# Token weights staged further ahead in a Fourier filter and mixer kernel, with readerless matmuls, joint copies and adds on VectorE

## The chip, the cores and the metric

The kernel runs on one core of a Trainium2 chip. The metric is the device time of one execution in microseconds (us). Beside the profile of one execution there are the times of three plain runs.

## The reference

The input `x` has 8 batches of 3008 rows (the sequence) and 256 columns. Stage one multiplies its Fourier transform along the sequence by a complex filter; stage two is a mixer, first over the sequence ("token"), then over the columns ("channel"), with a residual in between. All is float32, except that the four mixer weights arrive as 64-bit floats.

```python
def _attn_ref(x, filt_r, filt_i):
    X = np.fft.rfft(x, axis=1)
    Y = X * (filt_r + 1j * filt_i)[None, :, :]
    return np.fft.irfft(Y, n=x.shape[1], axis=1).astype(np.float32)

def _moe_ref(x, w_tok1, w_tok2, w_ch1, w_ch2):
    xt = x.transpose(0, 2, 1)
    h = np.maximum(xt @ w_tok1, 0.0) @ w_tok2        # (3008, 256) and (256, 3008)
    u = x + h.transpose(0, 2, 1)
    h2 = np.maximum(u @ w_ch1, 0.0) @ w_ch2          # (256, 1536) and (1536, 256)
    return (u + h2).astype(np.float32)
```

## The kernel before

The transform of length 3008 is split as 47 x 64. A first set of matmuls works over the 64, a second set over the 47 for each of 32 row pairs k, then the filter product and the same two steps backwards. The last inverse step is not done by itself: its matrix (`wai`, and `wai_t` for the weights) is applied together with the mixer's token product. The mixer's matmuls over 1536 channels use a seven-product scheme of block sums, so that VectorE (DVE) and GpSimd (POOL) add blocks around TensorE's (PE's) matmuls. PE does 128 x 128 stationary by up to 512 moving float32 columns. The program is written in the order in which each engine runs it; each engine waits only for what its next instruction needs. Batch 0 is brought up first, in a stage of its own; after that batches follow each other with the filter of the next beside the mixer of the present one.

What the first stage does, in the order of the program:

- **Row transform of batch 0.** Twelve x tiles are multiplied by `wa0` (L534) and copied by ScalarE (ACT) into the tile `turned` (L537). After the sixth and the twelfth, eight DVE transposes each (L651) turn the rows in it. `turned` and `wa0` share one tile of the pool `wcp`, whose single place is later taken by the channel weights (`both`, the list `chan`).
- **Pair loop**, 33 steps over k = 0..32. `b_unit(k)` multiplies row k of `turned` by a table (L666), and DVE multiplies the result by the filter (L671) once ACT has copied the filter's second half (`filt_double`, L255). `bi_unit(k-1)` does two matmuls of 256 columns (L680) into one PSUM bank; ACT copies the result (L690, helper `by_block`), and after each odd k ACT issues the write to `g_tmp` (L687). ACT also turns the tables (L262, L263). Filter loads go out on POOL's queue (L243 to L250) eight k ahead, tables (L583) on SP's.
- **Weight tiles**, 38 in all: 12 of `w_tok1`, 14 of `w_tok2` (indices 12 to 25), 2 of `w_ch1`, and 10 more (`LAST`) of the channel weights. A 64-bit tile is loaded into a staging place (`stage`; L347 on SP for the first twelve, L362 and L394, L405 on POOL), scaled by ACT (L283), and rebuilt as a float32 part `top` and a small `rest` by four DVE instructions (L285, L286, L289, L291). For `w_tok1` and the first six tiles of `w_tok2` PE then adds the two by two matmuls that accumulate (L329 with `top`, L330 with `rest`, helper `on_chip`) and ACT copies the sum out (L332); for the others DVE adds (L318). In the pair loop every two k end one tile; `convert_end` counts it in `ended` and calls `fill`.
- **How far ahead tiles begin.** `fill(5)` begins loads while fewer than five tiles (four for `LAST`) are begun and not ended; `pause` holds it for the last k of the loop. Staging places come from a list: 7 buffers `t4`, then six buffers (`u`, `t`, `v`, two each) in turn for indices 12 to 27, then `t2` and `t3`. A load into a place that was used before waits until DVE has read the older tile.
- **Token sums.** `t4_load` reads rows of `g_tmp` back (L782, on SP, three of the last ones on POOL), and 96 matmul records (L788) sum over the sequence. Then come the first units of u (L874, L882), which need all fourteen `w_tok2` tiles, and the mixer items (L975, L985, L1004, L1022 on PE; L953 is the helper of all DVE adds), between which the remaining tiles are converted and POOL combines channel weights (L382 to L386). The filter of batch 1 runs beside them: its `z_tmp` writes (L545), reads (L661, L662), filter loads (L229 to L235) and products (L707).

The matmuls of the pair loop and the adding of the two parts, before the change:

```python
            for i, p in enumerate(prods.pop(k)):
                wi = turn_i[:, k // WC % 4, k % WC] if i else wbs[k // WC][:, TI:TI + 2 * KR:2, k % WC]
                nc.tensor.matmul(ps[0:KR], wi, p, start=(i == 0), stop=(i == 1))
```

Of the kernel before, what the change touches and what calls it, by code (L numbers as in the profile page):

```python
# [10 lines left out]
FP32 = mybir.dt.float32  # L11
I64 = mybir.dt.int64
U32 = mybir.dt.uint32
AF = mybir.ActivationFunctionType
ALU = mybir.AluOpType
# [4 lines left out]
N1 = 47  # L20
N2 = 64
NF = N // 2 + 1
D = 256
P = 128
K2 = 32
A = 24
KR = 4 * A
# [3 lines left out]
NXC = A // XC  # L31
# [4 lines left out]
KC = 2  # L36
KD = 2 * KC
WC = 2
TI = P - 2 * KH + 1
DT = 256  # L40
TC = DT // P
DC = 1536
JT = DC // P
JP = JT // 2
DH = D // P
# [3 lines left out]
NG = 10  # L49
W2G = -(-N2 // NG)  # L50
# [80 lines left out]
def kernel(  # L131
# [11 lines left out]
    nc = tc.nc  # L143
# [23 lines left out]
    wcp = pool("wcp", 1)  # L167
# [6 lines left out]
    t4p = pool("t4p", A // TC4 + 1)  # L174
# [10 lines left out]
    def bank(tag):  # L185
        return (psg if tag == "pg" else psum).tile([P, 512], FP32, tag=tag, name="ps_" + tag)
# [5 lines left out]
    def free_bank():  # L192
        turn.reverse()
        return turn[0]
# [4 lines left out]
    wai_t = glob.tile([P, P], FP32, name="wai_t")  # L199
# [7 lines left out]
    w1 = w1_all[:, 0:A * DT].rearrange("p (a t) -> p a t", t=DT)  # L207
# [3 lines left out]

    w2m = [w2[:, t, 0:7 * 256].rearrange("p (s n) -> p s n", s=7) for t in range(2)]

    turned = wcp.tile([P, K2 * D + P], FP32, tag="wc", name="turned")
    wa0 = turned[:, K2 * D:]
    turned = turned[:, 0:K2 * D].rearrange("p (s d) -> p s d", d=D)
    chan = []


# [46 lines left out]

    early = [(up, "u")] * 2 + [(tp, "t")] * 2 + [(vp, "v")] * 2
    late = [(t2p, "t2"), (t3p, "t3")]
    stages = [(t4p, "t4")] * (A // 2) + (early * 3)[0:TC * W2G + DH] + late * 5

    def stage(n):
        where, tag = stages.pop(0)
        return where.tile([P, n], I64, tag=tag, name="st")

    def halves(st, n, pair):
# [45 lines left out]
    ended = [0]  # L321
    behind, banks = [], ["po%d" % i for i in range(4)]

    def on_chip(stat, top, rest, n, parts):
        banks.append(banks.pop(0))

        def f(tag=banks[0]):
            ps = bank(tag)
            nc.tensor.matmul(ps[:, 0:n], stat, top, start=True, stop=False)  # L329
            nc.tensor.matmul(ps[:, 0:n], stat, rest, start=False, stop=True)  # L330
            for src, dst in parts:
                nc.scalar.copy(out=dst, in_=src(ps))  # L332

        behind.append(f)

    def w1_tile(i):
        st = stage(512)
        rows = moe_w_tok1.rearrange("(n2 n1) t -> n2 n1 t", n1=N1)
        q = nc.sync if i < EARLY else nc.gpsimd
        if 2 * i + 2 == A:  # L340
            nc.gpsimd.memset(st.bitcast(U32)[:, 512:1024], 0)
        for j in range(2):
            a = 2 * i + j
            both = a + 1 < A
            src = bass.AP(tensor=rows.tensor, offset=rows.offset + (A - 1 - a) * DT,
                          ap=[[N1 * DT, N2]] + [[(1 + 2 * a) * DT, 2]] * both + [[1, DT]])
            q.dma_start(st[0:P:1 if both else 2, ts(j, DT)], src)  # L347
        yield

        h = halves(st, 512, spare_pair())  # L350
        yield next(h)
        yield next(h)
        on_chip(wai_t, *next(h), 512, [(lambda v: v, w1[:, 2 * i:2 * i + 2, :].rearrange("p a t -> p (a t)"))])

    def w2_load(i):

# [103 lines left out]
    begun, pause = [0], []  # L460

    def fill(ahead):
        while not pause and begun[0] < len(tiles) and begun[0] < ended[0] + (4 if begun[0] >= len(tiles) - len(LAST) else ahead):
            start()

    def start():
# [5 lines left out]
    xs, ahead = {}, []  # L472
# [92 lines left out]
    def dft(bs):  # L565
# [72 lines left out]
        for i, u in enumerate(() if tiled else todo):  # L638
            if first and i in (0, 2):
                w_load(i // 2)  # L640
            if first and i in (6, 8):
                table_load(i // 2 - 1)
            a_unit(*u)
            if bs != GROUPS[1] or i >= XB:
                more(1)
            yield "a" if i + 1 < len(todo) else "w"
            if first and (i + 1) % (NXC // 2) == 0:

                for d in range(i // (NXC // 2) * P, (i + 1) // (NXC // 2) * P, 16):
                    v = turned.rearrange("p s d -> p d s")[:, d:d + 16, :]  # L650
                    nc.vector.transpose(v, v)  # L651
        t2s, t3s, prods = {}, {}, {}
        def t2_load(c):
            t2s[c] = t2p.tile([P, KD, D], FP32, tag="t2", name="t2")
# [19 lines left out]
        def bi_unit(k):  # L674


            ps = bank(free_bank()).rearrange("p (b d) -> p b d", b=2)[:, 0:nb, :]
            for i, p in enumerate(prods.pop(k)):
                wi = turn_i[:, k // WC % 4, k % WC] if i else wbs[k // WC][:, TI:TI + 2 * KR:2, k % WC]
                nc.tensor.matmul(ps[0:KR], wi, p, start=(i == 0), stop=(i == 1))  # L680
            c, r = divmod(k, KC)
            if r == 0:
                where, tag = (p2p, "p2") if c % 3 == 2 else (t3p, "t3")
                t3s[c] = where.tile([KR, KC, nb, D], FP32, tag=tag, name="t3")
            by_block(t3s[c][:, r], ps[0:KR])
            if r == KC - 1:
                nc.scalar.dma_start(g_d[0][ts(c, KC)].rearrange("k r b d -> r k b d"), t3s.pop(c))  # L687

        def by_block(out, ps):
            nc.scalar.copy(out=out.rearrange("p b (e g i) -> p b g e i", e=DH, i=CW),  # L690
                           in_=ps.rearrange("p b (g e i) -> p b g e i", e=DH, i=CW))
# [695 lines left out]
```

## Time and profile before

| what | value |
|---|---|
| three runs, median (lowest to highest) | 2398.6 us (2395.35 to 2398.96) |
| the profiled execution | 2395.43 us, its span 2393.7 us |
| PE busy over the span | 2356.6 us, 98% |
| DVE, ACT, POOL busy | 1943.6, 688.1, 641.0 us |
| mean granted clock of PE | 0.996 |
| PE busy from 0 to 100, 100 to 200, 200 to 300 us | 82.5, 93.9, 96.2 us |
| DVE, ACT, POOL busy from 60 to 80 us, of 20 | 15.7, 17.7, 17.0 us |
| DMA over the span | 294 MB, mean 123 GB/s |

The page cuts the span into 40 slices of 60 us and gives the busy share of each in tenths. Tables by stretch give, for each engine, the busy time and the number of instructions, then the granted share of PE's clock, the mean busy share of the 16 DMA engines and what they moved in GB/s. A timeline row has the start, the length, the engine, the line, output and input, and in brackets the idle time of the engine ahead of it and what ended that. A row of waits has the total, how often, and the longest. Issuing a DMA is not counted as busy time of the engine that issues it, and a float32 matmul stands as two records.

### The profile page before, as it was taken

The page shows a single profiled execution, that of the slowest core. Times are in us where ns is not written, and L with a number is a line of the kernel's source. Part 1 is how long each engine was busy: PE and PEld are TensorE (multiplying, and loading weights), DVE is VectorE, ACT ScalarE, POOL GpSimd, SP SyncE. Part 2 cuts the span into 40 slices and gives each one's busy share as a digit, 9 for nine tenths or more (in the row PEclk, how much of TensorE's full clock was granted, in tenths as well). Part 3 has the DMA queues.
Part 4 walks back from the last instruction along what each step waited for, and adds up shares of the span by engine and source line. Part 5 has one row for each costly group of instructions (what it writes and reads, how often), then busy time and mean ns, then how long its engine had stood idle before and what let it go on. Part 6 is the DMA issues. An engine that isn't in the chain of part 4 may idle for free.

```text
span 2393.7 us, 36991 instructions
## 1 busy us (share of the span) xinstructions
PE 2356.6 (98%) x13108; PEld 2007.5 (84%) x13108; DVE 1943.6 (81%) x3653; ACT 688.1 (29%) x1339; POOL 641.0 (27%) x1124
## 2 busy tenths in 40 slices
PE   7999999999999999999999999999999999999998
PEld 4667789888898888988888888988889888898887
DVE  7797887888887888878887788788888788877776
ACT  5732222322223222232222222132222322212222
POOL 8485533211211121222111211221121112112121
PEclk8999999999999999999999999999999999999999
DMA  8864446333354333533344333533335433331100
GB/s 228 235 197 134 146 129 223 112 108 94 112 178 134 94 96 110 198 112 95 104 154 153 107 94 104 193 113 108 94 112 177 135 94 97 108 130 33 38 15 21
DMA packets 190423, 294.28 MB, mean 123 GB/s; under 512 B 34444, under 2 KB 124962, under 8 KB 190238
## 3 DMA queue, kind: packets, MB, share of 16 engines
q1 hardware_dynamic: 148750, 231.24, 31.1%
q0 software_dynamic: 34688, 53.83, 8.6%
q10 hardware_dynamic: 6800, 6.85, 0.9%
q8 instruction: 104, 1.70, 0.3%
q14 instruction: 81, 0.66, 0.1%
HBM read 209.06 MB, written 82.72 MB: 122 GB/s over the span
## 4 chain that ended last, share of the span: by engine, by line
PE 93%; DVE 3%; DMA 2%; issue 1%; POOL 1%; ACT 0%; SPq 0%; DVEq 0%; ACTq 0%; POOLq 0%
PE ps_po L1022 35%; PE ps_pg L975 20%; PE ps_pg L1004 15%; PE ps_b L527 3%; PE ps_b L839 3%; PE ps_acc L896 3%; PE ps_pg L527 2%; PE ps_acc L839 2%; PE ps_b L896 2%; PE ps_acc L874 2%; PE ps_b L874 2%; DVE t L953 1%; PE ps_pg L666 1%; DMA x<-in_x_dram 1%; PE ps_b L680 1%
## 5 line engine op out<-in xcount | busy, mean ns | idle before, releaser
L1030 POOL DMA_DIRECT2D out_dram<-r x752 | 408.3, 551 | 1452.1 <-issue 864.0
L1009 ACT ACTIVATE hh<-hh 128x512 f32<-128x512 f32 (+1 forms) x568 | 342.7, 621 | 989.1 <-DVE hh L953 989.1
L953 DVE TENSOR_TENSOR hh<-ps_pg,s 128x512 f32<-128x512 f32 (+3 forms) x852 | 475.4, 585 | 167.2 <-ACT s L978 157.1
L1022 PE MATMUL ps_po<-t,wc 128*128 128x256 f32 (+1 forms) x2296 | 556.4, 379 | 0.8 <-DVE t L953 0.8
L1022 PEld LDWEIGHTS ps_po<-t,wc 128*128 128x128 f32 x2296 | 427.1, 190 | 93.0 <-issue 33.9
L1022 PE MATMUL ps_po<-hh,wc 128*128 128x256 f32 (+1 forms) x1722 | 411.5, 375 | 1.1 <-POOL wc L386 1.1
L975 PE MATMUL ps_pg<-v,wc 128*128 128x256 f32 (+1 forms) x1704 | 406.6, 375 | 0.0
L1022 PEld LDWEIGHTS ps_po<-hh,wc 128*128 128x128 f32 x1722 | 326.8, 190 | 40.2 <-POOL wc L386 1.9
L975 PEld LDWEIGHTS ps_pg<-v,wc 128*128 128x128 f32 x1704 | 323.5, 190 | 36.9 <-DVE v L953 0.4
L1004 PE MATMUL ps_pg<-u,wc 128*128 128x256 f32 (+1 forms) x1136 | 287.7, 376 | 3.3 <-DVE hh L953 3.1
L953 DVE TENSOR_TENSOR t<-t,hh 128x256 f32<-128x256 f32 (+1 forms) x576 | 247.6, 430 | 19.8
L1004 PEld LDWEIGHTS ps_pg<-u,wc 128*128 128x128 f32 x1136 | 213.9, 190 | 32.7 <-DVE hh L953 7.5
L953 DVE TENSOR_TENSOR s<-ps_pg,hh 128x512 f32<-128x512 f32 (+1 forms) x284 | 193.3, 681 | 29.6
L978 ACT COPY s<-ps_pg 128x256 f32<-128x256 f32 (+1 forms) x284 | 104.4, 367 | 326.5 <-PE ps_pg L975 326.4
L953 DVE TENSOR_TENSOR t<-hh 128x512 f32<-128x512 f32 (+1 forms) x288 | 194.4, 675 | 0.6 <-ACT hh L1009 0.6
L975 PE MATMUL ps_pg<-u,wc 128*128 128x256 f32 (+1 forms) x568 | 166.9, 375 | 0.4 <-DVE hh L953 0.4
L1004 PE MATMUL ps_pg<-v,wc 128*128 128x256 f32 (+1 forms) x568 | 166.4, 375 | 0.0
L975 PEld LDWEIGHTS ps_pg<-u,wc 128*128 128x128 f32 x568 | 106.3, 190 | 14.1 <-DVE hh L953 2.1
L1004 PEld LDWEIGHTS ps_pg<-v,wc 128*128 128x128 f32 x568 | 107.3, 190 | 12.7
L953 DVE TENSOR_TENSOR u<-ps_acc,u 128x256 f32<-128x256 f32 (+1 forms) x84 | 46.1, 549 | 72.4 <-PE ps_acc L896 50.2
L953 DVE TENSOR_TENSOR u<-ps_b,u 128x512 f32<-128x512 f32 (+2 forms) x126 | 74.5, 591 | 28.9 <-PE ps_b L896 26.7
L896 PE MATMUL ps_acc<-w 128*128 128x256 f32 (+1 forms) x336 | 85.2, 376 | 0.0
(168 smaller groups left out, 2708.4 us busy)
## 6 DMA issues: line engine op xcount, KB each, us to landing
w<-w_tmp SPq DMA_DIRECT2D x84, 448.0 KB
w<-w_tmp SPq DMA_DIRECT2D x35, 896.0 KB
out_dram<-r POOLq DMA_DIRECT2D x696, 32.0 KB, 3.5
g_tmp<-t SPq DMA_DIRECT2D x112, 192.0 KB
t<-g_tmp SPq DMA_DIRECT2D x42, 512.0 KB
t<-z_tmp SPq DMA_DIRECT2D x196, 96.0 KB
z_tmp<-t SPq DMA_DIRECT2D x72, 256.0 KB
wb<-wbi_t SPq DMA_DIRECT2D x56, 256.0 KB
```

The source lines that it names most:

```text
L527: nc.tensor.matmul(outs(i, j), stat(i, j), mov(i, j), start=True, stop=True)
L666: nc.tensor.matmul(ps, wbs[k // WC][:, 0:2 * P:2, k % WC], turned[:, k, :].unsqueeze(1), start=True, stop=True)
L839: nc.tensor.matmul(ps[:, at], w[:, n], mov, start=(j == 0 and i in (0, 2)), stop=(j == AP - 1 and i >= 5))
L874: nc.tensor.matmul(ps[:, ds(q * P, n)], t4[b, c][:, r, ts(dh, P)], wai[:, 0:n], start=(first and q == 0), stop=(not first and q == 3))
L896: nc.tensor.matmul(ps[:, ds(j * hw, hw)], h1[:, n, :], w2m[m % 2][:, at, 0:hw], start=(i < 2 and j == 0), stop=(j == len(todo) - 1))
L953: nc.vector.tensor_tensor(out=out, in0=in0, in1=in1, op=op)
L975: nc.tensor.matmul(ps[:, 0:hw], chan[0][:, jp, n, :], mov, start=True, stop=True)
L978: nc.scalar.copy(out=s[:, 0], in_=g[0][:, 0, 0:hw])
L1004: nc.tensor.matmul(ps[:, 0:hw], chan[0][:, jp, n, :], mov, start=True, stop=True)
L1009: nc.scalar.activation(out=hs, in_=hs, func=AF.Relu)
L1022: nc.tensor.matmul(po[i][:, j, 0:hw], chan[1][:, jp, n, :], mov, start=(jp == 0 and first == 1), stop=(jp == JP - 1 and last == 1))
L1030: q.dma_start(bass.AP(tensor=ob.tensor, offset=ob.offset + row * D + g * cw, ap=[[N1 * D, 32], [D if h else -D, n], [1, cw]]), blocks[ts(g ...
```

## The change

Five edits, all in the first stage of the program:

- The tile that holds `turned` and `wa0` gets the size of `both` and the name `early_wc`. The staging list now has, after the 7-buffer places of the first twelve tiles, the six buffers once; then three places behind `wa0` in `early_wc` (indices 18 to 20); then five places on top of `turned`, four of its rows each (indices 21 to 25); then two buffers again for the two `w_ch1` tiles. One swap puts the short tile (index 18) into the short third place.
- `fill` has a rule by stretches: four ahead for `LAST`; from twelve begun tiles on, 5 + min(max(ended - 2, 0) // 2, 6) ahead, so 7 at seven ended tiles and 11 from fourteen on; below that, what the caller says.
- `on_chip` can be called without `rest`; for every second tile of `w_tok1` (six of twelve) DVE adds `rest` to `top` in place and PE does one matmul, not two.
- After each of the last eight transposes a matmul of 384 columns reads the slice just turned, with `wa0` as its stationary; nothing reads its result.
- `bi_unit` puts the results for k and k + 1 into the two halves of one PSUM bank, and ACT copies both with one instruction after the second.

```diff
-    turned = wcp.tile([P, K2 * D + P], FP32, tag="wc", name="turned")
-    wa0 = turned[:, K2 * D:]
-    turned = turned[:, 0:K2 * D].rearrange("p (s d) -> p s d", d=D)
+    early_wc = wcp.tile([P, 2 * JP * 7 * P], FP32, tag="wc", name="turned")
+    wa0 = early_wc[:, K2 * D:K2 * D + P]
+    turned = early_wc[:, 0:K2 * D].rearrange("p (s d) -> p s d", d=D)
...
-    stages = [(t4p, "t4")] * (A // 2) + (early * 3)[0:TC * W2G + DH] + late * 5
+    stages = [(t4p, "t4")] * (A // 2) + early + [(early_wc, K2 * D + P + n * NG * N1) for n in (0, 2, 4)]
+    stages += [(early_wc, n * 4 * D) for n in range(5)] + early[0:DH] + late * 5
+    stages[A // 2 + W2G - 1], stages[A // 2 + 8] = stages[A // 2 + 8], stages[A // 2 + W2G - 1]
 
     def stage(n):
         where, tag = stages.pop(0)
+        if where is early_wc:
+            return where[:, ds(tag, min(2 * n, 2 * JP * 7 * P - tag))].bitcast(I64)
         return where.tile([P, n], I64, tag=tag, name="st")
...
-            nc.tensor.matmul(ps[:, 0:n], stat, top, start=True, stop=False)
-            nc.tensor.matmul(ps[:, 0:n], stat, rest, start=False, stop=True)
+            nc.tensor.matmul(ps[:, 0:n], stat, top, start=True, stop=rest is None)
+            if rest is not None:
+                nc.tensor.matmul(ps[:, 0:n], stat, rest, start=False, stop=True)
...
-        on_chip(wai_t, *next(h), 512, [(lambda v: v, w1[:, 2 * i:2 * i + 2, :].rearrange("p a t -> p (a t)"))])
+        top, rest = next(h)
+        if i % 2:
+            nc.vector.tensor_tensor(out=top, in0=top, in1=rest, op=ALU.add)
+            rest = None
+        on_chip(wai_t, top, rest, 512, [(lambda v: v, w1[:, 2 * i:2 * i + 2, :].rearrange("p a t -> p (a t)"))])
...
-        while not pause and begun[0] < len(tiles) and begun[0] < ended[0] + (4 if begun[0] >= len(tiles) - len(LAST) else ahead):
+        while not pause and begun[0] < len(tiles):
+            if begun[0] >= len(tiles) - len(LAST):
+                ahead = 4
+            elif begun[0] >= A // 2:
+                ahead = 5 + min(max(ended[0] - 2, 0) // 2, 6)
+            if begun[0] >= ended[0] + ahead:
+                break
             start()
...
                     nc.vector.transpose(v, v)
+                    if i + 1 == NXC:
+                        nc.tensor.matmul(bank("pg")[:, 0:384], wa0, turned[:, 0:24, d:d + 16], start=True, stop=True)
...
-            ps = bank(free_bank()).rearrange("p (b d) -> p b d", b=2)[:, 0:nb, :]
-            for i, p in enumerate(prods.pop(k)):
-                wi = turn_i[:, k // WC % 4, k % WC] if i else wbs[k // WC][:, TI:TI + 2 * KR:2, k % WC]
-                nc.tensor.matmul(ps[0:KR], wi, p, start=(i == 0), stop=(i == 1))
             c, r = divmod(k, KC)
             if r == 0:
                 where, tag = (p2p, "p2") if c % 3 == 2 else (t3p, "t3")
                 t3s[c] = where.tile([KR, KC, nb, D], FP32, tag=tag, name="t3")
-            by_block(t3s[c][:, r], ps[0:KR])
+                prods["out"] = bank(free_bank()).rearrange("p (r d) -> p r d", r=KC)
+            ps = prods["out"]
+            for i, p in enumerate(prods.pop(k)):
+                wi = turn_i[:, k // WC % 4, k % WC] if i else wbs[k // WC][:, TI:TI + 2 * KR:2, k % WC]
+                nc.tensor.matmul(ps[0:KR, r:r + 1], wi, p, start=(i == 0), stop=(i == 1))
             if r == KC - 1:
+                by_block(t3s[c][:, :, 0], ps[0:KR])
                 nc.scalar.dma_start(g_d[0][ts(c, KC)].rearrange("k r b d -> r k b d"), t3s.pop(c))
```

## The prediction

> **What bounds the kernel now.** I read the page's slices first, then a table by 20 us and by 5 us, then each engine's timeline up to 260 us, last the waits.
>
> ```profile
> PE   7999999999999999999999999999999999999998
> PEclk8999999999999999999999999999999999999999
> ```
> TensorE (PE) is full from the second slice of 60 us on and its clock is down only in the first. All that the change edits lies in the first 190 us, so the gain is bounded by PE's idle time there and by PE work taken out of it. In order of time, from PE's timeline:
>
> ```profile
> 31.44 2.06 PE L666 MATMUL ps_pg<-turned,wb 128*128 128x256 f32 x4 [11.60 <-issue]
> 36.44 1.02 PE L329 MATMUL ps_po<-both,wai_t 128*128 128x512 f32 x2
> 40.79 1.02 PE L329 MATMUL ps_po<-both,wai_t 128*128 128x512 f32 x2
> 111.00 20.96 PE L788 MATMUL ps_b<-t,w 128*128 128x256 f32 x96 [2.08 <-DMA t<-g_tmp]
> 210.85 1.13 PE L1004 MATMUL ps_pg<-u,wc 128*128 128x256 f32 x4 [2.67 <-DVE hh L953]
> ```
> PE waits 11.6 us for the row turns, then runs without a gap through the pair loop (a period of 4.35 us for two rows k and one weight tile, 36.44 to 40.79), and waits for the last `g_tmp` rows at 111.0. That moment, called T0, ends the first stage. One period of ScalarE (ACT) in the loop:
>
> ```profile
> 39.25 0.58 ACT L332 COPY w<-ps_po 128x512 f32<-128x512 f32 x1 [0.40 <-PE ps_b L680]
> 39.73 0.37 ACT L690 COPY t<-ps_b 96x256 f32<-96x256 f32 x1
> 40.12 1.04 ACT L255 COPY filt<-filt 64x1024 f32<-64x1024 f32 x1
> 41.19 0.54 ACT L262 COPY turn_i<-wb 64x192 f32<-64x192 f32 x1
> 41.76 0.56 ACT L263 ACTIVATE turn_i<-wb 64x192 f32<-64x192 f32 x1
> 42.34 0.69 ACT L283 ACTIVATE both<-st 128x512 f32<-128x512 f32 x1
> 42.94 0.35 ACT L690 COPY t<-ps_acc 96x256 f32<-96x256 f32 x1
> 43.31 0.31 ACTq L687 DMA_DIRECT2D g_tmp<-t  x1
> 43.66 0.58 ACT L332 COPY w<-ps_po 128x512 f32<-128x512 f32 x1 [0.38 <-PE ps_b L680]
> ```
> Start to start it is 4.41 us, and the 0.4 "idle" is the DMA issue at 43.31. ACT has no gap at all and falls behind PE by 0.06 us a period: the loop, which looks PE-bound, is ACT-bound as well, and its last `g_tmp` write is issued by ACT at 104.39. The DMA engines and their waits:
>
> ```profile
> 20.00:25.00 5.00, 0.00 (x0) 0.00 (x0) 5.00 (x6) 1.15 (x2) 4.76 (x11) 0.62 0.64 168
> 30.00:35.00 5.00, 3.56 (x8) 2.30 (x9) 3.56 (x6) 0.81 (x2) 4.35 (x9) 0.51 1.04 260
> 90.00:95.00 5.00, 5.00 (x20) 3.90 (x18) 3.48 (x7) 4.51 (x10) 0.54 (x1) 1.00 1.00 330
> ...
> PE ps_po L1022 <- POOL wc L386: 1.1, 2, 0.6
> ACT w L332 <- DMA t<-g_tmp: 1.2, 1, 1.2
> ...
> SPq L782 <- DMA g_tmp<-t: 15.7, 4, 8.6
> ```
> The clock (third number from the end) falls at about 21 us and is back at about 35. DMA (the last two) is full in most rows of 75 to 105 us; a `g_tmp` write then takes so long that SP waits 8.6 us for one, and ACT once waits for an older load to land before it may issue its write.
>
> **The change part by part.** The sum stands against the profiled execution, 2395.43 us (span 2393.7 and 1.7 around it). It is 3.2 under the median of the three runs, 2398.6, and beside the lowest, 2395.35; from the median all totals are 3.2 higher. What a measurement can tell from no change is about 0.2%, 4.8 us.
>
> *Readerless matmuls.* Eight of 384 columns. A 512-column one takes 0.86 (L329 to L330), a 256 one 0.43, so 0.65 each, 1.3 at half clock. The 16 transposes take 17.22 us on VectorE (DVE), 1.08 each, and the last eight free one slice every 1.08; seven matmuls run in PE's 11.6 us of idle time and cost nothing; without that wait they would be 4.6. The eighth needs the last transpose and stands before the first L666: +0.65. Against it, at half clock PE is full from about 24, so the clock should be up before 31, and L666 and L680 take 0.43 rather than 0.9. The first product (DVE, 32.75) stays where it is; the second waits for L286 in any case (34.41). What is left is 0.4 on PE: the first L329 ends its pair at 37.7, not 38.16. If the clock stays low the same point is 0.7 later instead.
>
> *Joint copies.* Two copies of 256 columns (0.39 and 0.37 to the next start) become one of 512; the nearest row is L332, 0.58, and the issue behind must wait for its end: 0.61. ACT's period becomes 4.41 - 0.76 + 0.61 = 4.26. Ends: 0.48 (L332 to its next) and 0.74, no gain. Also the first copy (35.31), which stood ahead of the filter doubling (35.71), goes away, and ACT, idle since 30.84, doubles and turns early. Its first L332 then waits for PE at 37.7, not for its own queue: 37.85 for 39.25, 1.4 earlier (0.25 with the clock low).
>
> *VectorE adds.* Six second matmuls of 0.86 go, 5.2 us of PE in the loop: on average 4.35 becomes 3.92. That is under ACT's 4.26, so it is ACT that sets the period and most of the 5.2 turns into PE waiting. DVE gets six adds of 0.69 (its own L291 at the same size); it idles 0.65 to 0.99 each period ahead of the product that waits for L255, which hides them. Without that idle time they cost 4.1. DVE's mean period would be 3.85.
> The three together: 1.4 at the start and 14 periods and the last copy at 0.15, 2.15. ACT issues the last write at 104.39 - 3.55 = 100.85.
>
> *Tiles begun ahead.* No instruction is added, but their place moves. By the fill rule, with `ended` counting one tile every two k: by the pause, 23 tiles are begun and not 18, and 27 rather than 21 right behind the loop. POOL runs ahead: it issued its last such load at 98.27 and then waited 10.1 us. Places of their own take away waits for buffers there (3.0 and 3.7 and 4.2 us before the loads at 89.25, 93.53 and 98.27), so that about nine more tiles are issued by 89. On POOL the filter loads stand behind up to two more issues of 0.55 each; they go out eight k, 17 us, ahead and land in 4 to 7, so that hides. The three `t<-g_tmp` of POOL stand behind tiles 23 to 26, seven issues of 0.55, in POOL's 10 us wait: nothing. SP's order is unchanged, but its table loads and `g_tmp` reads share the engines. Tiles 21 to 26 are 2.6 MB that ran at 110 to 120: 8 us at 330 GB/s. Free DMA time in the 5 us rows of 60 to 105 is 5.2 (0.72, 0.72, 0.75, 0.99 and 0.78 the rows that are not full), so 2.8 or more may stand before the last write and reads; but the load at 98.27, which stands there now, is gone. I take the middle of 0 and 2.8, a delay of 1.4; the far end is all 2.6 MB at the loop's 230 GB/s, 11.5. T0: 111.0 - 3.55 + 1.4 = 108.85.
>
> *Behind T0.* PE then has 21 us of token sums. DVE converts in order from 102 to 176 and loses 0.72, 1.02 and 2.46 us up to 117 to loads that had not come; with those in place it is over 4 us ahead of PE. So PE's waits of 0.16, 0.55, 0.57 and 0.39 (150 to 185 us, for DVE and for POOL's combines behind DVE) go: 1.67. What is late next is the wait of 2.67 at 210.85, where DVE stands in a filter product that waits for a load. That load follows the last `z_tmp` write, issued at 186.76 beside POOL's `w_tmp` writes (181.45); an earlier POOL gets those out of the way. Between 0 and 2.67 I take half, 1.3. The new `wc` tile may be written only after the last staged tile has been read, which DVE's order gives anyway. Later stages have no PE idle time and no edit.
>
> Sum: 2395.43 - 3.55 + 1.4 - 1.67 - 1.3 = 2390.3. Or: 2388.9 plus the delay.
>
> **The rivals.** *The loop's gain is lost to DMA.* The delay is 2.8 to 6.5: 2391.7 to 2395.4, taken as 2393. For it: the 8.6 us of SP. Against it: 96.26, where a read landed after 2.3 us with two tiles issued in the 7 us before. The clock staying low (1.1 later) also ends here, 2391.4.
>
> *ACT blocked at its own DMA issue; slower.* L687 waits for an older transfer to land (1.2 us with the issue, at 102). If the moved loads stand in front of the writes of the loop's last third, SP's reads behind these land as much later, and ACT waits for them with the loop's last copies queued behind. The price is the delay itself: from 6.5 us on nothing is gained, from 11.3 on it is over 0.2% slower, and at the far end, 11.5, it is 2400.4. For it: DMA full from 75 on, and transfers that land in about the order in which they were issued on whatever queue (tile at 85.67, write at 87.39: both at 95 to 96). Against it: nothing is issued between about 90 and the end of the loop.
>
> *Queues that take turns.* Were the small write and reads served beside the large loads, the delay would be 0: 2388.9. For it: the read at 96.26. Against it: the order of landing just told. The Trainium skill, page DMA: Bandwidth & Descriptors, section Queues, rings and completion order, says that each DMA engine goes round-robin between the queues that have work, a packet at a time; by that rule the last write would not stand behind POOL's tiles and this would be the time. The landings of this trace between 75 and 100 us do not agree with it, so the sum keeps a delay.
>
> **How the numbers follow.** Forecast (delay 1.4, 2390.3) 0.36; queues in turn (2388.9) 0.14; gain lost (2393) 0.31; ACT blocked (2400.4 at its end, some of it under 0.2%) 0.19. Faster by over 0.2% (under 2390.6) is nearly all of the first two, 0.48; slower by over 0.2% the upper part of the last, 0.16; the rest 0.36. The range: low end 2387, the sum with no delay, all of the 2.67 and a cheaper copy; high end 2400, near the far end of the delay. The forecast's own range is 2388 to 2393.
>
> **What would show it.** ACT's starts of L332 4.26 apart and six L329 without L330; PE with small gaps in the loop; eight matmuls of 384 columns at 24 to 32 and the clock up before 31; the last L687 near 100.9 and L788 near 108.9; no PE wait on POOL's L386. Wrong if L687 waits microseconds for a landing, if L788 starts at 111 or later, or if DVE's adds make PE wait at L329 by more than ACT's lead.

## The result, and the profile after

The changed kernel takes 2402.01 us (median of 15 runs, 2399.89 to 2407.32), the kernel before 2395.98 (15 runs beside them, 2394.43 to 2398.96). The ratio is 1.0027, with a 95% interval of 1.002 to 1.0034: slower by 0.27%. The forecast was 2390.3, the range 2387 to 2400; both missed. The profiled run of the changed kernel took 2401.22 us with a span of 2399.4, 5.7 more than the span before. Most lines have moved: L329, L330, L332, L680, L687, L690, L782, L788 and L1022 of before are now L333, L335, L337, L702, L705, L708, L800, L806 and L1040, and L362 and L394, where GpSimd (POOL) issues the loads of the `w_tok2` and `w_ch1` tiles, are L371 and L403. L666, L671, L882, L975 and L1004 are now L683, L688, L900, L993 and L1022, the helper L953 is L971 and the combine L386 is L395; in the runs below some lines stand a few places off these.

From the timeline of TensorE (PE) after (start, length, then the idle time ahead and what ended it):

```profile
31.20 0.88 PE L668 MATMUL ps_pg<-turned 128*128 128x384 f32 x2 [0.20 <-DVE turned L666]
...
36.07 1.02 PE L333 MATMUL ps_po<-both,wai_t 128*128 128x512 f32 x2
...
95.69 0.76 PE L702 MATMUL ps_b<-p,wb 128*96 128x256 f32 x2 [1.81 <-DVE p L688]
...
116.28 22.58 PE L806 MATMUL ps_b<-t,w 128*128 128x256 f32 x96 [7.56 <-issue]
139.55 1.98 PE L900 MATMUL ps_acc<-w,h 128*128 128x512 f32 x4 [0.69 <-ACT h L882]
...
172.62 1.13 PE L1040 MATMUL ps_po<-hh,wc 128*128 128x256 f32 x4 [0.42 <-POOL wc L395]
190.58 0.70 PE L993 MATMUL ps_pg<-u,wc 128*128 128x256 f32 x2 [0.41 <-DVE hh L971]
...
216.03 1.13 PE L1022 MATMUL ps_pg<-u,wc 128*128 128x256 f32 x4 [2.30 <-DVE hh L971]
```

And the line of before that L900 is held against:

```profile
132.64 1.99 PE L882 MATMUL ps_acc<-w,h 128*128 128x512 f32 x4 [0.69 <-ACT h L864]
```

The start is as planned: the readerless matmuls fill the wait, and the loop's first L333 stands at 36.07, 0.37 earlier than before. But T0, the start of the token sums, is 116.28 and not 111.0, and the sums take 22.58 us and not 20.96. These two, 5.28 and 1.62, are the 6.9 by which L900 is late (139.55, against 132.64 for L882 before). Behind it 1.2 comes back from shorter waits: 0.42, 0.41 and 2.30 in place of 0.16, 0.55, 0.57, 0.39 and 2.67. That is the 5.7 of the span.

ScalarE (ACT): one period early in the loop, and the end of the loop.

```profile
37.98 0.59 ACT L337 COPY w<-ps_po 128x512 f32<-128x512 f32 x1 [1.13 <-PE ps_po L335]
38.59 1.04 ACT L255 COPY filt<-filt 64x1024 f32<-64x1024 f32 x1
...
41.38 0.56 ACT L708 COPY t<-ps_acc 96x512 f32<-96x512 f32 x1
41.98 0.32 ACTq L705 DMA_DIRECT2D g_tmp<-t  x1
42.33 0.59 ACT L337 COPY w<-ps_po 128x512 f32<-128x512 f32 x1 [0.39 <-PE ps_po L333]
...
93.87 1.04 ACT L255 COPY filt<-filt 64x1024 f32<-64x1024 f32 x1 [1.90 <-DMA filt<-in_filt_i_dram]
...
97.20 0.31 ACTq L705 DMA_DIRECT2D g_tmp<-t  x1
...
101.93 0.31 ACTq L705 DMA_DIRECT2D g_tmp<-t  x1
...
104.21 0.31 ACTq L705 DMA_DIRECT2D g_tmp<-t  x1
```

ACT starts the loop 1.27 earlier (37.98 for 39.25), with a period of 4.35 and not 4.41 here; over the eleven periods to 86.63 the mean is 4.42, as one of them (72.93 to 77.94) is 0.65 longer. At 93.87 it waits 1.90 for a filter load, and the last `g_tmp` write goes out at 104.21, about where it was (104.39). Then the sums wait 12.07 us from that issue, 6.61 before. POOL's timeline has what was issued meanwhile:

```profile
90.19 0.55 POOL L243 DMA_DIRECT2D filt<-in_filt_r_dram  x1 [1.74 <-ACT both L287]
...
94.38 0.56 POOL L371 DMA_DIRECT2D turned<-in_moe_w_tok_dram  x1
95.73 2.66 POOL L371 DMA_DIRECT2D turned<-in_moe_w_tok_dram  x5 [0.79 <-DMA filt<-in_filt_r_dram]
98.38 1.02 POOL L403 DMA_DIRECT2D st<-in_moe_w_ch_dram  x2
101.88 0.49 POOL L403 DMA_DIRECT2D st<-in_moe_w_ch_dram  x1 [2.48 <-DMA turned<-in_moe_w_tok_dram]
103.77 0.57 POOL L403 DMA_DIRECT2D st<-in_moe_w_ch_dram  x1 [1.40 <-DMA turned<-in_moe_w_tok_dram]
```

Ten loads stand there, right in front of the last writes. Before, there was one, then POOL waited at its reads, and the DMA engines had room from 105 to 110 us:

```profile
98.27 0.54 POOL L362 DMA_DIRECT2D st<-in_moe_w_tok_dram  x1 [4.20 <-ACT t L690]
108.88 1.60 POOL L782 DMA_DIRECT2D t<-g_tmp  x3 [10.08 <-DMA g_tmp<-t]
105.00:110.00 5.00, 2.73 (x7) 1.00 (x6) 3.84 (x10) 3.33 (x9) 1.02 (x3) 1.00 0.40 115
```

The DMA engines by 5 us (clock third from the end, then DMA share and GB/s) and SP's wait between 90 and 116 us:

```profile
100.00:105.00 5.00, 4.60 (x17) 2.80 (x15) 4.86 (x11) 3.96 (x9) 1.06 (x2) 1.00 1.00 365
105.00:110.00 5.00, 3.29 (x8) 0.97 (x6) 3.87 (x10) 3.60 (x9) 0.00 (x0) 1.00 1.05 294
110.00:115.00 5.00, 0.00 (x0) 0.00 (x0) 4.79 (x13) 1.41 (x3) 0.94 (x2) 0.78 0.45 67
115.00:120.00 5.00, 3.72 (x10) 3.08 (x11) 4.83 (x11) 1.14 (x2) 1.99 (x6) 0.54 0.96 180
```
```profile
SPq L800 <- DMA g_tmp<-t: 17.0, 3, 10.2
```

DMA is full to 110 (its share from 105 to 110 was 0.40 before, with 115 GB/s), SP waits 10.2 us for one `g_tmp` write, PE does nothing from 110 to 115, and its clock falls with that. That wait ends at 106.93 and is, by its time, for the write of 97.20. The last write is slow too: in SP's timeline the first read behind it goes out at 113.64, 9.4 us after its issue, where the kernel before needs 4.0 (104.39 to 108.37) and e8, told below, 2.5. From that read to T0 it is 2.6 us in all three. So the write is what comes late, and not the reads behind it. What the queues moved from 102 to 105 us (packets, MB, share of the 16 engines; q0 is POOL's queue, and q10, by its bytes over the whole run, ACT's):

```profile
q0 software_dynamic: 175, 1.06, 85.3%
q10 hardware_dynamic: 168, 0.17, 16.1%
```

Both queues are served beside each other, with about as many packets each. But a packet of POOL's loads has 6 KB here and one of ACT's write 1 KB, so the write gets a seventh of the bytes. From 95.2 to 101.9 us ACT's queue moves no packet at all, although a write was issued at 97.20; why that one begins so late stays open.

### The profile page after: what moved, and what is told of

Read it like the earlier page. It is cut to its first block, busy times and chain, and to the rows that moved or that the text cites. A ratio compares the mean times of both kernels' runs of the same rounds, so it can differ in the third digit from the quotient of the medians.

```text
span 2399.4 us, 36973 instructions
## 1 busy us (share of the span) xinstructions
PE 2361.5 (98%) x13112; PEld 2009.1 (84%) x13112; DVE 1947.1 (81%) x3659; ACT 687.9 (29%) x1323; POOL 641.0 (27%) x1124
## 4 chain that ended last, share of the span: by engine, by line
PE 89%; DVE 1%; issue 0%; DMA 0%; ACT 0%; SPq 0%; DVEq 0%; ACTq 0%
PE ps_po L1040 35%; PE ps_pg L993 19%; PE ps_pg L1022 15%; PE ps_b L542 3%; PE ps_b L857 3%; PE ps_acc L914 3%; PE ps_pg L542 2%; PE ps_acc L857 2%; PE ps_b L914 2%; PE ps_acc L892 2%; PE ps_b L892 2%; DVE t L971 0%; PE ps_b L900 0%; PE ps_acc L900 0%; DVE hh L971 0%
## 5 line engine op out<-in xcount | busy, mean ns | idle before, releaser
L971 DVE TENSOR_TENSOR hh<-ps_pg,s 128x512 f32<-128x512 f32 (+3 forms) x852 | 475.1, 585 | 167.1 <-ACT s L996 157.0
L1040 PE MATMUL ps_po<-t,wc 128*128 128x256 f32 (+1 forms) x2296 | 556.5, 379 | 0.6 <-DVE t L971 0.6
L1040 PEld LDWEIGHTS ps_po<-t,wc 128*128 128x128 f32 x2296 | 427.0, 190 | 92.9 <-issue 34.6
L1040 PE MATMUL ps_po<-hh,wc 128*128 128x256 f32 (+1 forms) x1722 | 411.3, 375 | 0.4 <-POOL wc L395 0.4
L993 PE MATMUL ps_pg<-v,wc 128*128 128x256 f32 (+1 forms) x1704 | 406.6, 375 | 0.0
L1040 PEld LDWEIGHTS ps_po<-hh,wc 128*128 128x128 f32 x1722 | 326.9, 190 | 39.2 <-issue 1.2
L993 PEld LDWEIGHTS ps_pg<-v,wc 128*128 128x128 f32 x1704 | 323.5, 190 | 36.9 <-DVE v L971 0.4
L1022 PE MATMUL ps_pg<-u,wc 128*128 128x256 f32 (+1 forms) x1136 | 287.7, 376 | 2.9 <-DVE hh L971 2.8
L971 DVE TENSOR_TENSOR t<-t,hh 128x256 f32<-128x256 f32 (+1 forms) x576 | 247.7, 430 | 19.8
L1022 PEld LDWEIGHTS ps_pg<-u,wc 128*128 128x128 f32 x1136 | 213.8, 190 | 32.3 <-DVE hh L971 7.3
L971 DVE TENSOR_TENSOR s<-ps_pg,hh 128x512 f32<-128x512 f32 (+1 forms) x284 | 193.3, 681 | 31.7 <-DVE hh L971 2.8
L971 DVE TENSOR_TENSOR t<-hh 128x512 f32<-128x512 f32 (+1 forms) x288 | 194.5, 675 | 0.6 <-ACT hh L1027 0.6
L993 PE MATMUL ps_pg<-u,wc 128*128 128x256 f32 (+1 forms) x568 | 166.9, 375 | 0.4 <-DVE hh L971 0.4
L1022 PE MATMUL ps_pg<-v,wc 128*128 128x256 f32 (+1 forms) x568 | 166.4, 375 | 0.0
L993 PEld LDWEIGHTS ps_pg<-u,wc 128*128 128x128 f32 x568 | 106.3, 190 | 14.0 <-DVE hh L971 1.8
L1022 PEld LDWEIGHTS ps_pg<-v,wc 128*128 128x128 f32 x568 | 107.3, 190 | 12.7
L971 DVE TENSOR_TENSOR u<-ps_acc,u 128x256 f32<-128x256 f32 (+1 forms) x84 | 46.1, 549 | 73.0 <-PE ps_acc L914 50.5
L971 DVE TENSOR_TENSOR u<-ps_b,u 128x512 f32<-128x512 f32 (+2 forms) x126 | 74.4, 591 | 28.9 <-PE ps_b L914 26.7
```

Of the source, the lines that this page charges most:

```text
L971: nc.vector.tensor_tensor(out=out, in0=in0, in1=in1, op=op)
L993: nc.tensor.matmul(ps[:, 0:hw], chan[0][:, jp, n, :], mov, start=True, stop=True)
L1022: nc.tensor.matmul(ps[:, 0:hw], chan[0][:, jp, n, :], mov, start=True, stop=True)
L1040: nc.tensor.matmul(po[i][:, j, 0:hw], chan[1][:, jp, n, :], mov, start=(jp == 0 and first == 1), stop=(jp == JP - 1 and last == 1))
```

## The experiments

The theory after the result: (A) tile loads stand in front of the last write and reads, which land behind them; the rest of the change is a small gain. Against it: (B) the fall of the clock, (C) the late filter loads inside the loop, (D) one of the three other edits. "Last write" below is the issue of the last `g_tmp` write; it and T0 are from the profiled execution, while "us" is the median of the timed runs, with the ratio to the kernel before on the same chip.

| run | last write | T0 | sums take | us | ratio |
|---|---|---|---|---|---|
| before | 104.39 | 111.00 | 20.96 | 2395.98 | 1 |
| after | 104.21 | 116.28 | 22.58 | 2402.01 | 1.0027 [1.002, 1.0034] |
| e1 five ahead | 102.18 | 107.01 | 20.96 | 2393.22 | 0.9989 [0.9979, 0.9998] |
| e2 ahead alone | 106.47 | 117.41 | 22.38 | 2403.24 | 1.0035 [1.0024, 1.0046] |
| e3 reads first | 104.59 | 111.88 | 22.64 | 2395.73 | 1.0003 [0.9993, 1.0012] |
| e4 seven matmuls | 104.38 | 117.14 | 22.59 | 2398.72 | 1.0007 [0.9997, 1.0017] |
| e5 readerless | 104.66 | 110.41 | 20.96 | 2395.01 | 0.9994 [0.9985, 1.0002] |
| e6 joint copies | 102.73 | 109.58 | 20.96 | 2395.44 | 0.9994 [0.9985, 1.0003] |
| e7 adds | 103.66 | 109.95 | 20.96 | 2393.91 | 0.9989 [0.998, 0.9997] |
| e8 late ahead | 101.95 | 107.08 | 20.96 | 2392.67 | 0.999 [0.9981, 0.9999] |
| e9 nine matmuls | 102.70 | 114.80 | 20.88 | 2399.36 | 1.0017 [1.0007, 1.0026] |
| e10 two more | 107.15 | 113.00 | 20.88 | 2397.2 | 1.0 [0.9991, 1.0009] |
| e11 at loop end | 107.70 | 115.44 | 23.10 | 2402.69 | 1.0029 [1.0019, 1.004] |

**e1, the changed kernel with the old rule of five.**

```diff
-        while not pause and begun[0] < len(tiles):
-            if begun[0] >= len(tiles) - len(LAST):
-                ahead = 4
-            elif begun[0] >= A // 2:
-                ahead = 5 + min(max(ended[0] - 2, 0) // 2, 6)
-            if begun[0] >= ended[0] + ahead:
-                break
+        while not pause and begun[0] < len(tiles) and begun[0] < ended[0] + (4 if begun[0] >= len(tiles) - len(LAST) else ahead):
             start()
```

> The changed kernel with the old rule for how far ahead tiles begin (five), the places of their own and the other three edits kept. Theory A (the loads begun further ahead stand in front of the last g_tmp write and its reads): the last write lands in about 4 us again and not 9, the filter load that made ScalarE wait 1.9 us at 92 comes in time, so the token sums start at 107 to 109 and the time is 2 to 4 us under the kernel before. Theory B (the joint copies, the adds and the readerless matmuls cost it): the time stays 5 to 7 us over the kernel before, with the sums starting at 114 or later.

PE's timeline of it:

```profile
107.01 20.96 PE L800 MATMUL ps_b<-t,w 128*128 128x256 f32 x96 [0.29 <-DMA t<-g_tmp]
```

With the four other edits left in and only the number ahead put back, T0 is 9.27 earlier than in the changed kernel and the time 8.8 less, as theory A expected. The loss is in the tiles begun ahead, and D falls.

**e2, the staging alone on the kernel before** (the places and the new rule of `fill`, none of the other three edits).

> The kernel before with the places and the new rule of up to eleven tiles ahead alone. Theory A: the delay of the reads comes back by itself, sums at 115 to 118, 4 to 8 us slower than before. Theory B: within 2 us of before.

T0 is 117.41, and the ratio, 1.0035, is not told apart from that of the whole change. Here ACT stands still twice for DMA: 1.59 us ahead of its copy of 95.20, until a `g_tmp` write has landed, and 0.66 for a filter load. So the staging by itself costs 7.6 us (2403.24 to 2395.64, the kernel before on that chip), as much as the whole change or more.

**e3, the changed kernel with the last reads ahead of the fill behind the loop.**

```diff
-        fill(5)
         for c in range(A // TC4):
             t4_load(0, c, PARTS[3], P, (nc.sync, nc.gpsimd)[c % 2])
+        fill(5)
```

> The changed kernel with the fill behind the loop moved behind the last reads of g_tmp, so that POOL begins four tiles (indices 23 to 26) only after its own reads. Theory A: most of the delay goes, since seven of POOL's nine loads of 94 to 104 us are no longer in front: sums at 109 to 111, time 0 to 3 us under before. If instead the loads begun inside the loop are enough for the delay, the sums stay at 114 or later and the time at 4 us or more over before.

POOL now issues only three tiles at 93.9 to 97 and then waits 10.46 us for its reads; the rest follow them. T0 moves from 116.28 to 111.88, 4.4 earlier, though the filter load is as late as in the changed kernel (2.19 us at 93.79) and the last write 0.4 later. The same loads, behind the reads, cost less: that is A. The expected 109 to 111 and 0 to 3 us under the kernel before were narrowly missed; the sums take 22.64 here as well, after a wait of PE of 3.00. What is left against e1, 4.9 of T0 (2.4 of it in the last write), goes with the tiles begun within the loop.

**e4 and e9, PE kept busy while it waits.** Ahead of the token sums 7 (e4) or 9 (e9) matmuls of 512 columns whose result nothing reads.

```diff
                 sum_up()
+                for _ in range(7):
+                    nc.tensor.matmul(bank("pg"), wai, filts[0].rearrange("p i k d -> p (i k d)")[:, 0:512], start=True, stop=True)
```

> The changed kernel with seven more readerless matmuls of 512 columns on TensorE ahead of the token sums, 6 us of work in a wait of 7.6. If the clock's fall in that wait is worth the 1.6 us by which the token sums took longer (22.6 for 21.0), the sums take 21 again and the time is 1.6 us under the changed kernel, still 4 us over before. If the sums' length comes from late reads, nothing changes.

> The changed kernel with nine readerless matmuls of 512 columns, not seven, ahead of the token sums, so that TensorE waits less than 1 us between its last tile and the sums. Theory (the clock falls because TensorE waits for the reads, and that costs the sums 1.6 us): the clock stays full through 105 to 120, the sums take 20.96 and not 22.58 us, the time is 1 to 2 under the changed kernel's 2402. Rival (the clock falls for another reason, or a fall costs nothing that isn't given back): sums of 22.6, or the same time.

PE's timelines, e4 and then e9:

```profile
108.76 6.17 PE L1328 MATMUL ps_pg<-filt,wai 128*128 128x512 f32 x14
117.14 22.59 PE L806 MATMUL ps_b<-t,w 128*128 128x256 f32 x96 [2.21 <-issue]
```
```profile
107.07 7.89 PE L1328 MATMUL ps_pg<-filt,wai 128*128 128x512 f32 x18
114.80 20.88 PE L806 MATMUL ps_b<-t,w 128*128 128x256 f32 x96
```

In e4's profiled run a wait of 2.21 is left, the clock is at 0.51 from 117.0 to 120.5, and the sums still take 22.59. In e9's no wait is left, the clock is full throughout, and they take 20.88. So B is real: the idle PE costs the sums 1.7. It is also the smaller part, as e9 is still 0.17% slower than the kernel before. (It is 2.6 under the changed kernel and not 1 to 2; in its profiled run the last write goes out 1.5 earlier as well.) e4's median is 3.3 under the changed kernel although its profiled run saved nothing; that run (2401.45) is the slowest of its ten, so the others may have kept their clock, but no profile shows it. With the same loads in the same order, the changed kernel, e4 and e9 have the last write between 102.70 and 104.38, but from there to T0 always 12.1 to 12.8 us: the delay behind the last write is steady, and what scatters is the loop.

**e5, e6, e7, the other three edits one at a time on the kernel before.**

> The kernel before with the eight readerless matmuls alone. Theory (the loop's pace is set by ScalarE's 4.41 us a period and by the place of its first copy in its queue): the clock is full at about 27.5 instead of 34.9, PE's first pair ends 0.4 earlier, but ScalarE's first copy to w stays within 0.4 of 39.25; the last g_tmp write within 0.4 of 104.39 and the time within 0.5 of the kernel before. Rival (the clock's return is what brought the early start): first copy near 38.0, last write near 103.1, time about 1.3 under the kernel before.

> The kernel before with the joint inverse copies alone. Theory (two bounds on the loop lie side by side: ScalarE 4.41 and PE 4.35 a period): ScalarE falls to 4.36, PE stays at 4.35, so the loop's period gains at most 0.06; the first copy to w comes up to 1 us earlier, and the last write is at 103.0 to 104.0; time 0.3 to 1.3 under the kernel before. Rival (the joint copy's gain is 0.15 a period as predicted and PE follows): last write near 101, 3 us under.

> The kernel before with VectorE's six adds alone. Theory (ScalarE's 4.41 us sets the period): 5.2 us of PE go and come back as waits, last write within 0.5 of 104.39, time within 0.5 of the kernel before. Rival (PE sets the period, 4.35 against ScalarE's 4.41 being within the reading): last write 1 to 2.5 earlier and as much off the time. Third: the adds delay VectorE's products, and the write is later by up to 4.1, the six adds of 0.69.

*Readerless matmuls:* L332 starts at 39.04, 0.21 earlier, so ACT's own queue held it, as the theory said; the clock's share of full speed is 0.67 at 26 to 30 us and 1.00 at 30 to 35 (0.51 before); 1.1 us under the kernel before (0.5 was allowed), not told apart from it. *Joint copies:* ACT's period is 4.36 and L332's first start 38.74; the last write is 1.66 earlier, more than the 0.4 to 1.4 that the theory gave, since the kernel before has a wait of 1.19 at 102.37 there that here is 0.61. At 211 us the profile has a wait of 3.44, which gives some of it back: 0.7 us under the kernel before is left, within the 0.3 to 1.3 expected and not told apart from it. *Adds:* the loop's pace stays (39.17 to 43.60 is 4.43), and PE's waits on L356 rise to 2.9 us in all. Still the last write is 0.73 and T0 1.05 earlier and the time 2.2 less, so "within 0.5" fell, and the first rival is nearer; its profile lacks the 1.19 us wait for a landing that the kernel before has at 102. The three gains add to 3.06 of T0 and 4.1 us; together (e1, e8) they are 3.9 to 4.0 of T0 and 2.4 to 3.5 us. Nothing in these sums points to one edit needing another, and none is large.

**e8, five ahead until the last reads are issued, then the new rule.** A list `reads_out` gets its entry behind the last `t4_load`:

```diff
+            ahead = 5
             if begun[0] >= len(tiles) - len(LAST):
                 ahead = 4
-            elif begun[0] >= A // 2:
+            elif reads_out:
...
+        reads_out.append(True)
+        fill(5)
```

> The changed kernel, but tiles are begun only five ahead until the last reads of g_tmp have been issued; from then on up to eleven ahead as in the change. If what costs is only that tile loads stand in front of the last write and reads, the token sums start near 107.0 as in the run with five everywhere (2393.2 us), and the loads brought forward then take away what is left of PE's waits up to 190 us (1.15, 0.56, 0.40 and 0.26 there): 2391 to 2392.5. If the loads behind the reads collide with the reads all the same (they are served beside them), the sums start near 109 to 112 and the time is 2394 to 2397. If PE's later waits are not waits for late tiles, it is 2393.2, as with five.

```profile
107.08 20.96 PE L807 MATMUL ps_b<-t,w 128*128 128x256 f32 x96 [0.60 <-DMA t<-g_tmp]
...
154.03 1.13 PE L1041 MATMUL ps_po<-hh,wc 128*128 128x256 f32 x4 [0.55 <-POOL wc L395]
163.04 1.13 PE L1041 MATMUL ps_po<-hh,wc 128*128 128x256 f32 x4 [0.57 <-POOL wc L395]
181.00 0.70 PE L994 MATMUL ps_pg<-u,wc 128*128 128x256 f32 x2 [0.40 <-DVE hh L972]
```

It has the lowest median of all, 2392.67, 0.1% under the kernel before, but e1 at 2393.22 is not told apart from it. The reason is in POOL's timeline: in both runs POOL waits at its first read of `g_tmp` (14.20 us here, 15.15 in e1) and right behind the reads issues the same eight loads, at 106.7 to 110.4 here and 107.0 to 110.7 there. POOL has nothing between them, so beginning them earlier in program order, behind the reads, changes no issue. The waits of 0.55, 0.57 and 0.40 stay, although DVE's one wait from 113 to 182 us, of 1.0, is not for a load, and POOL makes its combines from 146.95 to 153.93 without a gap: they are POOL's and DVE's own work, not late tiles.

**e10, at most seven ahead.**

```diff
-                ahead = 5 + min(max(ended[0] - 2, 0) // 2, 6)
+                ahead = 5 + min(max(ended[0] - 2, 0) // 2, 2)
```

> The changed kernel with tiles begun at most seven ahead, not eleven. Theory (a dose: each load in front of the last write and reads delays them by its bytes): the sums start between 107.0 (five ahead) and 116.3 (eleven), by the number of extra loads near 110, no fall of the clock or a short one, time 2394 to 2397. Rival (a threshold: DMA time that was free takes up two loads): sums at 107 to 108 and 2392 to 2393.5. Rival (any tile of the new order in the loop makes the filter loads late, whatever the number): loop as slow as in the changed kernel, last write 104, sums 112 or later.

ACT's timeline:

```profile
104.94 0.31 ACTq L705 DMA_DIRECT2D g_tmp<-t  x1
105.30 0.95 ACT L337 COPY w<-ps_po 128x240 f32<-128x240 f32 x2 [4.48 <-DMA g_tmp<-t]
107.15 0.31 ACTq L705 DMA_DIRECT2D g_tmp<-t  x1
```

POOL's loads are out by 93.8, and ACT waits for no filter load in this stretch. But a write issued at 96.13 is followed by one that may be issued only at 104.94: ACT stands 4.48 us, the issue of 0.3 included, until an older transfer has landed, with the copies behind it, and the last write is at 107.15. Two more ahead cost about what the other edits bring: the ratio is 1.0. In this profiled run they cost 6.0 of the 9.3 us of T0 that the rule of eleven costs (113.0 against 107.0 in e1), in the medians 4.0 of 8.8 (2397.2 against 2393.2). DMA time that was free for two loads, the first rival, did not show; whether the dose is linear one profile does not show.

**e11, five ahead in the loop, all the extra loads when it is over, ahead of the reads.** As e8, but the list gets its entry at the end of the pause, ahead of `fill(5)`.

> The changed kernel with tiles begun five ahead in the pair loop, and all the extra ones begun when the loop is over, ahead of the last reads in program order. GpSimd can issue them from about 90 on, where it is idle. Theory (two separate costs: late filter loads in the loop, 2 us, and loads in front of the last write and reads, 7 us): no wait for a filter load at 93, last write near 102.2, but the sums start at 112 to 115 with the clock fallen, time 2397 to 2400. Rival (the loop's extra loads are what delays all else): sums at 107 to 109, 2392.5 to 2394.

POOL's and ACT's timelines:

```profile
88.97 3.18 POOL L371 DMA_DIRECT2D turned<-in_moe_w_tok_dram  x6 [1.58 <-DMA filt<-in_filt_r_dram]
...
99.83 0.49 POOL L403 DMA_DIRECT2D st<-in_moe_w_ch_dram  x1 [0.80 <-DMA turned<-in_moe_w_tok_dram]
113.50 1.25 POOL L801 DMA_DIRECT2D t<-g_tmp  x2 [13.18 <-DMA t<-g_tmp]
```
```profile
100.55 0.31 ACTq L706 DMA_DIRECT2D g_tmp<-t  x1
...
107.70 0.31 ACTq L706 DMA_DIRECT2D g_tmp<-t  x1
108.05 0.95 ACT L337 COPY w<-ps_po 128x240 f32<-128x240 f32 x2 [5.26 <-DMA t<-g_tmp]
```

ACT waits for no filter load (DVE's product at 98.28 stands 2.48 us for a DMA, but the write of 100.55 follows the one of 95.84 at the usual 4.7). That write is 1.4 earlier than its like in the changed kernel (101.93), and ACT then stands 5.26 us at its last issue, the issue included. T0 is 115.44 and the time that of the changed kernel. e8 and e11 differ only in whether the extra loads stand behind or ahead of the reads in program order: 8.4 of T0 and 10.0 us. That settles that the place of the loads is the cause. The way it acts differs: in e11 5.75 of the 8.4 lie ahead of the last write's issue, where ACT stood, and 2.6 behind it, while in the changed kernel ACT did not stand there and most of the loss lies behind the issue. What decides between the two stays open. C is seen in the changed kernel (ACT's 1.90; e8's last write is 2.26 earlier) but isn't needed for the loss. The expected "last write near 102.2" fell, as ACT was held.

## Why the prediction was wrong, point by point

- **Readerless matmuls: right.** Eight, of which the last ends at 32.1; the clock is full from 27.4 (34.9 before); the pair L333, L335 stands 0.37 earlier (0.4 foreseen).
- **Joint copies: right in kind, the size off.** The first L337 is 37.98 (37.85 foreseen, 39.25 before). The joint copy to its issue takes 0.60 (0.61 foreseen). But the period is 4.35, not 4.26: the step "0.48, L332 to its next" was mis-sized. That was the gap to a copy out of PSUM; with L690 gone, L337 is followed by L255, which reads SBUF, and it starts 0.61 later (37.98 to 38.59). The trace of before had a row for that: L690 (0.37 long) to L255, 0.39, with no overlap, while L332 (0.58 long) was followed by a PSUM copy after 0.48. In the mean over the loop even less came: e8, without the late loads, has 4.37 (38.17 to 86.23, eleven periods) for 4.41 before (39.25 to 87.75), a gain of 0.04 a period where 0.15 was foreseen. (Fourteen periods and one copy at 0.15 are 2.25 and not the 2.15 of the sum, which changes nothing here.)
- **Adds: right for the pace.** PE waits for them 2.5 us in all in the loop; ACT sets the pace. That they bring 2.2 us by themselves (e7) was not foreseen and is explained only in part.
- **T0 without a delay: right by luck.** 111.0 - 3.55 is 107.45; e8 has 107.08 and e1 107.01. But the last write was to go out at 100.85 and goes out at 101.95 and 102.18, and from it to T0 it is 5.13 and 4.83, not the 6.61 of the kernel before that the sum kept. The two errors cancel.
- **"I take the middle of 0 and 2.8, a delay of 1.4": this step failed.** Against 107.45 the delay was 8.8, of which 3.4 stand ahead of the last write's issue (104.21 for 100.85) and 5.5 behind it (12.07 for 6.61), and the clock fall 1.6 that no term had. Three sentences under it were wrong. "About nine more tiles are issued by 89": POOL issues in order and waited for its own older loads and for buffers, so that six of them went out at 94.38 to 98.4 and four more loads to 104.3. "On POOL the filter loads ... that hides": the last group of filter loads went out from 90.19 on (79.54 before), the one before it from 82.90 (75.03), and ACT lost 1.90. And "seven issues of 0.55, in POOL's 10 us wait: nothing": only POOL's time was priced there. That wait at the reads held back the loads behind it while the last writes and reads went through; once loads are put ahead of it, DMA is full at that moment. The far end, 2.6 MB with no free time to take them (11.5), was nearer to what came about: six tiles of `w_tok2` and four of `w_ch1`, 5 x 470 + 188 + 4 x 128 KB, are 3.1 MB, and at the 294 to 365 GB/s of these rows that is 8.5 to 10.5 us, an estimate that leaves out what else those rows moved.
- **Order of landing.** The rival "ACT blocked at its own DMA issue; slower" had the direction and priced the loss by the delay. Its threshold, 0.2% slower from a delay of 11.3 on, was too high: at 8.8 the profiled run is 0.24% slower, as the clock and the gains that did not come behind T0 add to the delay. In the changed kernel's trace the blocked engines are SP (10.2 us) and POOL; ACT was blocked in e2, e10 and e11. The time of "queues that take turns" did not come. The Trainium skill, page DMA: Bandwidth & Descriptors, section Queues, rings and completion order, says that each DMA engine goes round-robin between its queues. The trace agrees with that rule: 175 and 168 packets of POOL's and ACT's queues from 102 to 105 us, and in e11 138, 140 and 138 of POOL's, SP's and ACT's from 100 to 104. What failed is the step from turns to no delay, since turns were taken by packets, and a write in packets of 1 KB beside loads in packets of 6 KB got a seventh of the bytes. The trace of before had this as well (50 packets of POOL's queue and 58 of ACT's from 92 to 93 us, 0.31 and 0.06 MB), so that a tile and a write which land together there need not be served in the order of issue. With the loads ahead, T0 is 8.4 later than with them behind (e11 against e8).
- **The clock behind a wait** had no term. A wait of PE of 7.56 us took the clock to half (0.54 from 115 to 120) and cost 1.62. The Trainium skill, page TensorE: Matmul & The Clock Gate, Part 1, warns of idle gaps above about 3.4 us. The waits of 7.56 and 6.23 (e2) agree; but after 2.21 us (e4) and 3.00 (e3) the clock fell as well, while after 2.08 (before) it did not.
- **Behind T0: half right.** 1.67 was to go; 0.16 and 0.55 went, 0.57 and 0.39 became 0.42 and 0.41: 0.84. The latter are not waits for tiles (e8).
- **The wait of 2.67 at 210.85** became 2.30, not 1.3. It is 1.05 to 3.44 in the runs here, so that its scatter is as large as the term.

The account: 2388.9, the sum without a delay, plus 8.8 (T0) and 1.6 (clock), plus 0.8 and 0.9 of gains that did not come behind T0, is 2401.0; the profiled run took 2401.22. It adds up because each term is taken from that run's own trace.

## What to carry to other kernels

An engine's wait in front of a dependent read can be what keeps the DMA engines free for that read: before filling it with prefetches, count their bytes against the critical write and read, not only the issuing engine's time. Where all queues are full, a prefetch belongs behind the critical transfers in program order, and on an in-order issuing engine "further ahead" puts it in front of whatever follows there. Compare packets as well as bytes: in these traces a queue's share of full DMA engines went by packets, so that a small write in small packets fared worst. For a copy's pace, take the gap from a row with the same kind of successor.

## What had not been expected of the hardware

- With POOL's loads under way, SP could read behind the last 192 KB `g_tmp` write of ACT's queue 9.4 us after its issue (the changed kernel); with the loads behind the reads it was 2.5 us (e8). The queues were served packet by packet in turn, 175 and 168 packets in 3 us, though one's had 6 KB and the other's 1 KB.
- ACT lost 4.48 and 5.26 us at one DMA issue (e10, e11), the issue of 0.3 included, until an older transfer had landed, with its copies queued behind.
- PE's clock went to half after a wait of only 2.21 us in e4; four matmuls behind a wait of 2.62 us in e10 took 2.07 us and not 1.13, while behind the 2.67 us of the kernel before and 3.10 in e2 they took 1.13. The length of the wait alone does not decide in this range; what does is open.
